# Attention scores of later token groups: two groups at once in four 64x64 tiles, values in the same visit

## The chip, the cores and the metric

The kernel runs on one core of one Trainium2 chip. The metric is the device time of one execution in microseconds (us); the time before is the median of three runs. The profile comes from one more execution, taken by the hardware profiler.

## The reference

Window attention, then two gated feed-forward layers, all in float32. Queries and keys come as 4 batches x 8 heads x 576 positions x 64 numbers; a query sees itself and the 63 positions before it.

```python
scores = scale * np.matmul(q, k.transpose(0, 1, 3, 2))
mask = (rel >= 0) & (rel < window)          # window = 64
scores = np.where(mask, scores, -1000000000.0)
attn = np.exp(scores - np.max(scores, axis=-1, keepdims=True))
attn = attn / (np.sum(attn, axis=-1, keepdims=True) + 1e-09)
x = np.matmul(attn, v)                      # 2304 tokens x 512
x = (h * sigmoid(1.702 * h)) @ w_out        # h = x @ w_in, 2048 wide
out = (silu(xn @ w_gate) * (xn @ w_val)) @ w_o2   # xn = x / rms * rms_g, 1536 wide
```

## The kernel before

The 2304 tokens are 36 groups of 64. A group's queries see two blocks of 64 keys: the group's own and the one before it. Heads are taken in four pairs, so a group's scores are a tile of 128 rows (two heads x 64 queries) by 4 x 128 columns (four head pairs, 128 keys each).

Stage A (to about 425 us) holds the attention and the first feed-forward layer. The tokens go in six blocks of 512, 256 and four times 384. For each block there are 16 steps; step c multiplies the block by 128 columns of `w_in` (`up`, L652 to L654) and the result by 128 rows of `w_out` (`down_t`, L737 to L739). Each operand is split into a high and a low part in a reduced float32 form, so a product is three matmuls. Stage B is the second layer (from L1071 on, to the end of the program).

The attention of groups 0 to 7 (block 0) stands at the start. That of groups 8 to 35 is strewn between the steps of the block before the one that needs it. For each such group `attention` issues:

- the scores (L490): four matmuls in full float32, 128 x 128 into 128 columns. To get two heads from one matmul, the queries are stored as a block-diagonal matrix, half of it zeros: 64 rows of one head against 64 columns, 64 rows of the other against the other 64. The profile counts each such matmul as two instructions, since full float32 goes in two half passes, each with its own weight load.
- on VectorE the mask (L517) and the row maximum (L522), on ScalarE the exponentials (L527), on VectorE the inverse sums, on GpSimd or ScalarE the normalising product;
- the turning of the weights: for groups below 18 by TensorE transposes (L545), from 18 on by VectorE's transpose (L573) and copies of 32 x 32 blocks.

`values` (L619) then multiplies two groups' weights with their values: 16 matmuls of 128 x 64 into 64 columns, head one to the lower 64 output rows, head two to the upper ones. From its bank ScalarE makes the high part of x and VectorE the low part (L631), which `up` reads.

TensorE's output lives in 8 banks: four accumulators `y0` to `y3`, two in a ring `bank` (for `up`), two in a ring `abank` (scores, transposes, values, row sums). A ring gives out its tiles in turn, each when its last user is done.

The order of all instructions is made before the run: every operation is handed to `Planner.op` with a cost for each engine that could do it, its dependences and a priority (in steps of stage A). `Planner.emit` walks a simulated time and writes down which operation each engine takes next. Costs of going from one form of matmul to another are in `Planner.TURN` (r: reduced float32, f: full float32, v: values). On the chip each engine then runs its list in that order and waits on semaphores. SyncE issues most loads, in its list's order. The weights arrive as float64 and are made float32 by VectorE and ScalarE (`w_narrow`, L391 to L405), and then split (`w_split`, L436) in stage A.

Of the kernel before, what the change touches and what calls it, by code (L numbers as in the profile page):

```python
# [9 lines left out]
F32 = mybir.dt.float32  # L10
F32R = mybir.dt.float32r
# [31 lines left out]
class Planner:  # L43
# [180 lines left out]
def dma(nbytes):  # L224
    c = Load(0.45)
    c.size = nbytes
    return c
# [3 lines left out]
def window_attention_two_moe_kernel(ctx: ExitStack, tc: tile.TileContext, ins, out):  # L231
    nc = tc.nc
    qh, kh, vh, w_in, w_out, w_gate, w_val, w_o2, rms_g = ins
    NBAT, NBLK = qh.shape[0], qh.shape[1]
    NT, DM = out.shape
# [80 lines left out]
    pl = Planner({k: v[1] for k, v in KINDS.items()})  # L316

    pts = [at.tile([P, NK, P], F32, name=f"pts{i}") for i in range(2)]
    KS = 8
# [8 lines left out]
    def make(b):  # L328
        if b.kind == "pt":
            turn = pt_turn[0] = 1 - pt_turn[0]  # L330
            b.tile = pts[turn]
            return b.tile
        if b.kind in mix_turn:
# [110 lines left out]

    q_of, kw, vw, vals = {}, {}, {}, []
    starts = [("keys", n) for n in range(KS // 2)]

    def wkey(g):
        b, i = divmod(g, NBLK)
        return b, max(i - 1, 0)  # L450

    def load_q(g, prio, kind="q", by="D"):
        b, i = divmod(g, NBLK)
        t = q_of[g] = Buf(kind)
        pl.op({by: dma(P * 2048)}, lambda e: (nc.scalar if e == "A" else nc.sync).dma_start(out=make(t), in_=qh[b, i]),
              prio, new=[t], size=P * 2048)

    def load_k(g, prio, kind="k"):
        if wkey(g) in kw:
            return  # L460
        b, i = wkey(g)
        t = Buf(kind)
        kw[b, i] = (lambda: t.tile), [t]
        pl.op({"D": dma(P * 2048)}, lambda e: nc.sync.dma_start(out=make(t), in_=kh[b, :, i:i + 2]), prio, new=[t])

# [14 lines left out]
    def attention(g, p0, step, ekind="e", ptkind="pt", norm=("G",), ptev=("A", "V"), hi=("A",)):  # L480
# [70 lines left out]
        if g < NS:  # L551
            pl.op({"T": 1.2}, masked_scores, p0, r=[*qk, "mask", "negative", "ident", *extra],
                  w=["scores order"], new=[sb],
                  mode="f")
            pl.op({"V": dve(512)}, highest_of, p0, r=[sb], new=[nb])
# [33 lines left out]
        return g, v, pb, [v, pb, "at", *extra] + (nov if g >= NPE else []), hi  # L589

    turns = {}
    idle = Buf("y2")
    idles = []

    def stay_warm(n, after):
        first = not idles

        def fn(e):
            t = make(idle) if first else idle.tile
            for _ in range(n):  # L600
                nc.tensor.matmul(t[:, 0:P], warm, warm, start=True, stop=True)

        idles.append(pl.op({"T": 0.25 * n}, fn, -70, r=["warm", START], after=[after], mode="f",
                           **({"new": [idle]} if first else {"hold": [idle]})))
# [786 lines left out]
    warm = start.tile([P, P], F32, name="warm")  # L1391
    n_first = start.tile([P, 1, P], F32R, name="n_first")
    n_rest = start.tile([P, 1, P], F32R, name="n_rest")
    ident_r = start.tile([P, P], F32R, name="ident_r")
    first_exp = start.tile([P, 1], F32, name="first_exp")
# [19 lines left out]
    pl.op({"G": 0.1}, lambda e: nc.gpsimd.memset(mhalf, -0.5), -97, w=["mhalf"])  # L1415

    def load_k_start(i, prio):
        tok = starts[i // 2]
        pl.op({"D": dma(P * 2048)}, lambda e: nc.sync.dma_start(out=k_start[:, i:i + 2], in_=kh[0, :, i:i + 2]), prio, w=[tok])

# [104 lines left out]
    plans.sort()  # L1525
    parts, pending = [], []
    pi = 0
    bi = 0
    for s in range(SA):
        j, c = steps[s]  # L1530
        while pi < len(plans) and plans[pi][0] <= s:
            p, g = plans[pi]
# [9 lines left out]
        while pending and s >= first[next(i for i in range(NBA) if gbase[i] + ngrp[i] > pending[0][0][0][0]) - 1]:  # L1542
            values(*pending.pop(0))
        gs, o = a_up(j, c, s)
# [88 lines left out]
```

## Time and profile before

| | us |
|---|---|
| median of three runs | 903.09 (902.3 to 903.85) |
| the profiled execution | 902.74 |
| its span, first to last instruction | 901.0 |
| TensorE busy in the span | 892.7 |
| VectorE busy | 677.5 |
| ScalarE busy | 446.8 |
| GpSimd busy | 287.6 |

A matmul's line names its output tile, then its operands, the shape of the weights and that of the result. Matmuls overlap in the profile: a busy time of one is longer than the distance from its start to the next start, so distances between starts are what a matmul costs in a dense stream. Idle time of TensorE is listed with what ended it.

### The profile page before, as it was taken

The page shows a single profiled execution, that of the slowest core. Times are in us where ns is not written, and L with a number is a line of the kernel's source. Part 1 is how long each engine was busy: PE and PEld are TensorE (multiplying, and loading weights), DVE is VectorE, ACT ScalarE, POOL GpSimd, SP SyncE. Part 2 cuts the span into 40 slices and gives each one's busy share as a digit, 9 for nine tenths or more (in the row PEclk, how much of TensorE's full clock was granted, in tenths as well). Part 3 has the DMA queues.
Part 4 walks back from the last instruction along what each step waited for, and adds up shares of the span by engine and source line. Part 5 has one row for each costly group of instructions (what it writes and reads, how often), then busy time and mean ns, then how long its engine had stood idle before and what let it go on. Part 6 is the DMA issues. An engine that isn't in the chain of part 4 may idle for free.

```text
span 901.0 us, 15907 instructions
## 1 busy us (share of the span) xinstructions
PE 892.7 (99%) x5656; PEld 845.6 (94%) x5656; DVE 677.5 (75%) x1320; ACT 446.8 (50%) x1106; POOL 287.6 (32%) x414
## 2 busy tenths in 40 slices
PE   9999999999999999999999999999999999999998
PEld 8888889999999999999999999998999999999998
DVE  6999986667657666764459888888787867677896
ACT  7975665566655666564337444444432224322251
POOL 4211212243444444541002543233222224233440
PEclk9999999999999999999999999999999999999999
DMA  9952455636556455533356999999998879988992
GB/s 333 394 200 75 124 190 182 233 120 223 199 182 208 158 177 158 190 136 117 133 189 245 347 348 337 328 327 285 377 369 268 259 202 296 287 248 234 260 226 71
DMA packets 96020, 208.03 MB, mean 231 GB/s; under 512 B 8754, under 2 KB 45380, under 8 KB 94404
## 3 DMA queue, kind: packets, MB, share of 16 engines
q1 hardware_dynamic: 68148, 145.40, 46.2%
q0 software_dynamic: 27648, 61.35, 23.4%
q8 instruction: 45, 0.74, 0.3%
q14 instruction: 35, 0.29, 0.1%
q10 hardware_dynamic: 144, 0.26, 0.1%
HBM read 147.20 MB, written 59.78 MB: 230 GB/s over the span
## 4 chain that ended last, share of the span: by engine, by line
PE 91%; DVE 4%; ACT 3%; DMA 1%; issue 1%; POOL 0%; SPq 0%; POOLq 0%; DVEq 0%; ACTq 0%
PE bank L1071 9%; PE bank L1072 9%; PE bank L1073 9%; PE y L737 7%; PE y L739 7%; PE y L738 7%; PE bank L652 7%; PE bank L653 7%; PE bank L654 7%; PE abank L490 3%; PE y L1346 2%; PE y L1345 2%; PE y L1347 2%; PE abank L619 2%; PE abank L1345 1%; PE abank L1346 1%
## 5 line engine op out<-in xcount | busy, mean ns | idle before, releaser
L1071 PE MATMUL bank<-slab,slab 128*128 128x384 f32 x456 | 154.6, 339 | 0.8 <-DVE gh L1110 0.8
L1072 PE MATMUL bank<-slab,slab 128*128 128x384 f32 x456 | 153.7, 337 | 0.8 <-DVE slab L931 0.8
L1073 PE MATMUL bank<-slab,slab 128*128 128x384 f32 x456 | 153.5, 337 | 0.0
L737 PE MATMUL y<-gh,slab 128*128 128x384 f32 (+2 forms) x384 | 132.0, 344 | 0.4 <-DVE y L761 0.4
L739 PE MATMUL y<-gh,slab 128*128 128x384 f32 (+2 forms) x384 | 129.1, 336 | 0.0
L652 PE MATMUL bank<-xh,slab 128*128 128x384 f32 (+2 forms) x380 | 128.9, 339 | 0.2 <-DVE mix L720 0.2
L738 PE MATMUL y<-gl,slab 128*128 128x384 f32 (+2 forms) x384 | 129.0, 336 | 0.0
L654 PE MATMUL bank<-xh,slab 128*128 128x384 f32 (+2 forms) x380 | 127.9, 336 | 0.0
L653 PE MATMUL bank<-xl,slab 128*128 128x384 f32 (+2 forms) x380 | 127.8, 336 | 0.0
L960 POOL DMA_DIRECT2D slab<-wc x96 | 55.7, 581 | 179.0 <-PE bank L1073 173.6
L1071 PEld LDWEIGHTS bank<-slab,slab 128*128 128x128 f32 x456 | 85.6, 188 | 8.7 <-DVE gh L1110 2.8
L1072 PEld LDWEIGHTS bank<-slab,slab 128*128 128x128 f32 x456 | 85.7, 188 | 5.9 <-DVE slab L931 1.0
L720 DVE SCALAR_TENSOR_TENSOR mix<-mix,bank 128x384 f32<-128x384 f32 (+2 forms) x95 | 52.1, 549 | 49.2 <-ACT mix L716 48.7
L1073 PEld LDWEIGHTS bank<-slab,slab 128*128 128x128 f32 x456 | 85.6, 188 | 0.0
L716 ACT ACTIVATE mix<-bank 128x384 f32<-128x384 f32 (+2 forms) x95 | 46.3, 488 | 78.9 <-PE bank L654 77.4
L1110 DVE TENSOR_TENSOR gh<-gl,bank 128x384 f32<-128x384 f32 x108 | 59.2, 550 | 24.9 <-PE bank L1073 24.2
L737 PEld LDWEIGHTS y<-gh,slab 128*128 128x128 f32 x384 | 72.2, 188 | 3.5 <-DVE y L761 0.6
L739 PEld LDWEIGHTS y<-gh,slab 128*128 128x128 f32 x384 | 72.1, 188 | 2.7
L738 PEld LDWEIGHTS y<-gl,slab 128*128 128x128 f32 x384 | 72.2, 188 | 2.5
L652 PEld LDWEIGHTS bank<-xh,slab 128*128 128x128 f32 x380 | 71.5, 188 | 3.2 <-DVE mix L720 0.5
L654 PEld LDWEIGHTS bank<-xh,slab 128*128 128x128 f32 x380 | 71.4, 188 | 2.7
L653 PEld LDWEIGHTS bank<-xl,slab 128*128 128x128 f32 x380 | 71.5, 188 | 2.6
(240 smaller groups left out, 2000.4 us busy)
## 6 DMA issues: line engine op xcount, KB each, us to landing
slab<-wc POOLq DMA_DIRECT2D x72, 512.0 KB, 5.1
wc<-slab SPq DMA_DIRECT2D x36, 512.0 KB, 6.0
wp<-raw SPq DMA_DIRECT2D x24, 512.0 KB, 3.6
fw<-wp SPq DMA_DIRECT2D x12, 1024.0 KB, 8.4
q<-in_q_dram SPq DMA_DIRECT2D x35, 256.0 KB, 4.6
raw<-in_w_in_dram SPq DMA_DIRECT2D x16, 512.0 KB, 8.2
raw<-in_w_out_dram SPq DMA_DIRECT2D x16, 512.0 KB, 6.5
k<-in_k_dram SPq DMA_DIRECT2D x25, 256.0 KB, 3.7
```

Of the source, the lines that this page charges most:

```text
L652: nc.tensor.matmul(h, w[:, 0, kk], xh_ring[:, kk, at_], start=(kk == 0), stop=False)
L653: nc.tensor.matmul(h, w[:, 0, kk], xl_ring[:, kk, at_], start=False, stop=False)
L654: nc.tensor.matmul(h, w[:, 1, kk], xh_ring[:, kk, at_], start=False, stop=(kk == NK - 1))
L720: nc.vector.scalar_tensor_tensor(out=th, in0=th, scalar=1.0, in1=hb.tile[:, 0:n], op0=ALU.add, op1=ALU.mult)
L737: nc.tensor.matmul(y, s[:, 0, cols], hb.tile[:, 0:n], start=first, stop=False)
L738: nc.tensor.matmul(y, s[:, 0, cols], lb.tile[:, 0:n], start=False, stop=False)
L739: nc.tensor.matmul(y, s[:, 1, cols], hb.tile[:, 0:n], start=False, stop=last)
L960: pl.op({"G": 0.6}, lambda e: nc.gpsimd.dma_start(out=frame(f)[:, :, 0:n], in_=d), prio, r=[key], w=tok, size=P * 8 * n)
L1071: nc.tensor.matmul(h, w[:, 0, kk], xh[:, kk], start=kk == 0, stop=False)
L1072: nc.tensor.matmul(h, w[:, 0, kk], xl[:, kk], start=False, stop=False)
L1073: nc.tensor.matmul(h, w[:, 1, kk], xh[:, kk], start=False, stop=kk == 1)
L1110: nc.vector.tensor_tensor(out=(make(to) if kind else s.tile)[:, 0:HT].bitcast(F32), in0=s.tile[:, 0:HT].bitcast(F32), in1=b.tile[:, 0:HT], ...
```

## The change

Groups 8 to 35 are no longer taken one by one but as 14 pairs (g, g + 1), g even.

- **Queries.** They come dense, not block-diagonal: 64 rows hold the even heads of the pairs, 64 rows the odd heads. One load of 256 KB brings both groups (before 256 KB for each), and one of 384 KB the three key blocks that a pair needs (before 256 KB per group, shared by two groups where a batch begins).
- **Scores.** 16 matmuls of 64 x 64 into 128 columns replace eight of 128 x 128. Even heads use array rows 0 to 63 and write to one `abank`, odd heads rows 64 to 127 and write to the other, so that a pair holds both banks. Four tiles of the array take turns in the order (row half, column half) = (0,0), (1,1), (0,1), (1,0).
- **After the scores** each bank (four heads of both groups, 128 x 512) runs through the same chain as a group did before: mask, maximum, exponentials, inverse, product, transposes. The counts on VectorE, ScalarE and GpSimd stay, but for first groups of a batch, whose mask is now two instructions of half the size where only one group of the pair is first, and for eight block copies fewer.
- **Values** are 16 matmuls of the same form as before, into a `bank` instead of an `abank`. Their priority is set just behind the scores of the next pair, and a new form "s" (scores) in `TURN` lets the planner put both into one visit.
- **Loads.** Values are loaded for every group (28 loads of 256 KB; before, two groups at a batch's start shared one). The first pair's queries and keys wait for the last scores of the start (`opened`). There is one buffer for the pair's queries and one for its keys.
- The first pair is planned three steps later; masks of the start move into unused columns of `xl_ring`.

```diff
-    TURN = {("r", "v"): 0.071, ("f", "v"): 0.071, ("v", "r"): 0.233, ("v", "f"): 0.18}
+    TURN = {("r", "v"): 0.071, ("f", "v"): 0.071, ("v", "r"): 0.233, ("v", "f"): 0.18, ("r", "s"): 0.071, ("f", "s"): 0.071,
+            ("s", "r"): 0.233, ("s", "f"): 0.18, ("v", "s"): 0.071, ("s", "v"): 0.071}
...
-        "q": (at, 2, [P, NK, 2 * W], F32),
-        "k": (at, 1, [P, 2, NK, W], F32),
+        "q": (None, 2, [P, NK, 2 * W], F32),
+        "qq": (None, 1, [P, NK, 2 * W], F32),
+        "k": (None, 1, [P, 3, NK, W], F32),
...
-        "e": (at, 1, [P, NK, P], F32),
+        "e": (None, 2, [P, NK, P], F32),
...
+    def load_pair(g, prio):
+        t = q_of[g] = Buf("qq")
+        pl.op({"D": dma(P * 2048)}, lambda e: nc.sync.dma_start(
+            out=make(t).rearrange("p k c -> p (k c)"), in_=qp[g // 2].rearrange("p i k c -> p (i k c)")), prio, new=[t], after=opened)
+        t2 = k_of[g] = Buf("k")
+        pl.op({"D": dma(P * 3072)}, lambda e: nc.sync.dma_start(out=make(t2), in_=kh[:, g - 1:g + 2]), prio, new=[t2], after=opened)
...
+    def attention_pair(g, p0, step, norm=("G",), ptev=("A", "V")):
+        q, kb = q_of.pop(g), k_of.pop(g)
+        banks, es = [Buf("abank") for _ in range(2)], [Buf("e") for _ in range(2)]
...
+            for i in range(2):
+                for h in range(2):
+                    for lane, half in ((0, 0), (1, 1), (0, 1), (1, 0)):
+                        rows, p = slice(lane * W, (lane + 1) * W), 2 * h + half
+                        nc.tensor.matmul(to[lane][half * W:(half + 1) * W, (2 * i + h) * P:(2 * i + h + 1) * P],
+                                         qt[rows, i, p], kb.tile[rows, i:i + 2, p], start=True, stop=True)
+
+        pl.op({"T": 1.0}, scores, p0, r=[q, kb], w=["scores order"], new=[*banks, *es],
+              after=[vals[NS - 1], idles[-1]], mode="s")
+        chains = [half_chain(g, lane, p0, step, banks[lane], es[lane], firsts, norm, ptev) for lane in range(2)]
+        return g, v_of.pop(g), chains
...
+    def values_pair(part, prio):
+        g0, vs, chains = part
+        ob = Buf("bank")
...
+                        pt = chains[j][0].tile[:, 2 * i + p // 2, p % 2 * W:(p % 2 + 1) * W]
+                        nc.tensor.matmul(o[rows, (p * 2 + i) * W:(p * 2 + i + 1) * W], vt, pt, start=True, stop=True)
...
     def plan(j, s0, s1):
-        for i in range(ngrp[j]):
-            plans.append((s0 + i * (s1 - s0) / ngrp[j], gbase[j] + i))
+        n = ngrp[j] // 2
+        for i in range(n):
+            plans.append((s0 + i * (s1 - s0) / n, gbase[j] + 2 * i, s0 + (i + 1) * (s1 - s0) / n - 0.28))
...
-        plan(j, first[j - 1] - 2, first[j] - 2)
+        plan(j, first[j - 1] - (2 if j > 1 else -1), first[j] - 2)
...
-            load_q(g, p - 4)
-            load_k(g, p - 4)
-            if wkey(g) not in vw:
-                load_v(g, p - 3, ("v", "t1" if g < NPE else "vx")[len(vw) % 2], ups[-2:-1])
-            parts.append(attention(g, p - 0.3, 1.7, norm=("A", "G") if g < gbase[2] else ("G",)))
-            if g % 2:
-                pending.append((parts, p - 0.3 + 2.5))
-                parts = []
+            load_pair(g, p - 4)
+            load_values(g, pv - 5, ("v", "t1" if g < NPE else "vx"), ups[-2:-1])
+            pending.append((attention_pair(g, p - 0.3, 1.7, norm=("A", "G") if g < gbase[2] else ("G",)), pv))
```

What this does to the order is shown at three places. A row is a line, an operation, output<-operands and the output's shape; "waits" names whose semaphores the instruction waits for.

**TensorE at the end of the start**, from the values of group 7 to the first matmuls of `up`. Before (L619 values, L490 scores of group 8, L652 to L654 `up`):

```order
L619 MATMUL abank<-pts_88,v_467 64x64 [waits DMAHW7_49,Activation_49]
L619 MATMUL abank<-pts_88,v_467 64x64 x7
L490 MATMUL abank<-k,q 128x128 [waits DMAHW6_49,DMAHW4_49,DVE_49]
L490 MATMUL abank<-k,q 128x128 x3
L652 MATMUL y_531<-xh,slab_510 128x256 [waits Activation_49]
L653 MATMUL y_531<-xl,slab_510 128x256 [waits DVE_49]
```

and of the changed kernel (L769 values, L638 the scores of the pair 8, 9, L802 to L804 `up`):

```order
L769 MATMUL abank<-pts_92,v_463 64x64 [waits DMAHW6_49,DVE_49]
L769 MATMUL abank<-pts_92,v_463 64x64 x7
L638 MATMUL abank<-kq,q 64x128 [waits DMAHW3_49,DMAHW4_49,DVE_49,PE_49]
L638 MATMUL abank<-kq,q 64x128 [waits DVE_49]
L638 MATMUL abank<-kq,q 64x128 x14
L802 MATMUL y_527<-xh,slab_506 128x256 [waits Activation_49]
L803 MATMUL y_527<-xl,slab_506 128x256
```

The second score matmul, the first that writes to the second bank, has a wait on VectorE of its own, and `up` behind it no longer has one.

**VectorE at the same place.** Before (L631 is the low part of x of groups 6 and 7, L405, L395 and L399 convert weights, L517 is the mask of group 8):

```order
L631 TENSOR_TENSOR xl<-abank,xh 128x4x64 [waits Activation_49]
L405 SCALAR_TENSOR_TENSOR raw_430<-raw_430 128x512 [waits DVE_49]
L395 TENSOR_SCALAR raw_495<-raw_495 128x512 [waits DMAHW1_49]
L395 TENSOR_SCALAR raw_514<-raw_514 128x512 [waits DMAHW2_49]
L399 SCALAR_TENSOR_TENSOR raw_495<-raw_495 128x512 [waits DVE_49]
L631 TENSOR_TENSOR xl<-abank,xh 128x4x64 [waits Activation_49]
L517 SCALAR_TENSOR_TENSOR e<-abank,m_rest 128x512 [waits PE_49]
```

and of the changed kernel (L781 low parts, L424 and L418 conversions, L653 the mask of the pair's first bank):

```order
L781 TENSOR_TENSOR xl<-abank,xh 128x4x64 [waits Activation_49]
L1590 TENSOR_SCALAR gcol<-gcol 128x4 [waits DMAHW1_49]
L424 SCALAR_TENSOR_TENSOR raw_410<-raw_410 128x512 [waits DVE_49]
L418 SCALAR_TENSOR_TENSOR raw_437<-raw_437 128x512
L781 TENSOR_TENSOR xl<-abank,xh 128x4x64 [waits Activation_49]
L653 SCALAR_TENSOR_TENSOR es_89<-abank,m_rest 128x256 [waits PE_49]
L653 SCALAR_TENSOR_TENSOR es_89<-abank,m_first 128x256
L424 SCALAR_TENSOR_TENSOR raw_437<-raw_437 128x512 [waits DVE_49]
```

The low part of group 7 keeps its place, and the mask stands right behind it in both, with weight conversions behind the mask.

**TensorE inside a block of 384.** Before, a value visit with one group's scores behind it (the other group's scores stand alone some 50 rows later):

```order
L654 MATMUL bank<-xh,slab_1116 128x384
L619 MATMUL abank<-pts_89,mix 64x64 x8
L619 MATMUL abank<-pts_88,v 64x64 x8
L490 MATMUL abank<-k,q 128x128 x4
L737 MATMUL y_2505<-gh,slab_1147 128x384
```

and of the changed kernel (L723 values, of which 16 rows of this kind follow each other, four shown; L887 `down_t`):

```order
L804 MATMUL bank<-xh,slab_1028 128x384
L638 MATMUL abank<-kq,q 64x128 x16
L723 MATMUL bank<-pts_93,v 64x64
L723 MATMUL bank<-pts_92,v 64x64
...
L723 MATMUL bank<-pts_93,mix 64x64
L723 MATMUL bank<-pts_92,mix 64x64
L887 MATMUL y_2528<-gh,slab_1076 128x384
```

All of a pair's scores now stand in one place. Of the 14 pairs' score visits, eight have a value visit right behind them as here; six stand alone, the first pair's among them, and six value visits stand alone. The order of stage B is the same in both kernels.

## Rows read from the trace of the kernel before

**Rows 1.** The page's busy times and granted TensorE clock over 40 slices

```profile
PE 892.7 (99%) x5656; PEld 845.6 (94%) x5656; DVE 677.5 (75%) x1320; ACT 446.8 (50%) x1106; POOL 287.6 (32%) x414
...
PEclk9999999999999999999999999999999999999999
```

**Rows 2.** Waits of TensorE, 0 to 425 us: total us, times, longest; first and last

```profile
PE y L1403 <- DVE warm L1396: 1.0, 1, 1.0
...
PE bank L652 <- DVE mix L720: 0.2, 1, 0.2
```

**Rows 3.** The line of the scores: count, least, median and longest duration in ns

```profile
L490 PE MATMUL abank<-k,q x224: 270/275/377, 29.4 to 391.5; 128*128 128x128 f32 x112
```

**Rows 4.** Timeline of TensorE around one score visit: start, busy, line, form, count

```profile
109.50 0.39 PE L739 MATMUL y<-gh,slab 128*128 128x512 f32 x1
109.72 1.05 PE L490 MATMUL abank<-k,q 128*128 128x128 f32 x8
...
110.85 0.39 PE L653 MATMUL bank<-xl,slab 128*128 128x512 f32 x1
111.08 0.39 PE L654 MATMUL bank<-xh,slab 128*128 128x512 f32 x1
```

**Rows 5.** Timeline of TensorE around one value visit

```profile
99.89 0.39 PE L654 MATMUL bank<-xh,slab 128*128 128x512 f32 x1
100.21 0.69 PE L619 MATMUL abank<-pts,v 128*64 128x64 f32 x16
100.72 0.64 PE L619 MATMUL abank<-pts,t 128*64 128x64 f32 x16
...
101.63 0.40 PE L738 MATMUL y<-gl,slab 128*128 128x512 f32 x1
```

**Rows 6.** Timeline of a value visit behind which a score visit stands

```profile
164.20 1.16 PE L490 MATMUL abank<-k,q 128*128 128x128 f32 x8
165.12 0.36 PE L652 MATMUL bank<-xh,slab 128*128 128x256 f32 x1
```

**Rows 7.** TensorE's timeline cut at 100.24 and 100.345 us (values), 109.75 and 109.85 us (scores)

```profile
100.21 0.28 PE L619 MATMUL abank<-pts,v 128*64 128x64 f32 x2
...
100.21 0.34 PE L619 MATMUL abank<-pts,v 128*64 128x64 f32 x4
...
109.72 0.27 PE L490 MATMUL abank<-k,q 128*128 128x128 f32 x1
...
109.72 0.38 PE L490 MATMUL abank<-k,q 128*128 128x128 f32 x2
```

**Rows 8.** Timeline of TensorE at the end of the start

```profile
29.45 1.16 PE L490 MATMUL abank<-k,q 128*128 128x128 f32 x8
30.84 0.38 PE L652 MATMUL y<-xh,slab 128*128 128x256 f32 x1 [0.24 <-ACT xh L356]
31.46 0.38 PE L653 MATMUL y<-xl,slab 128*128 128x256 f32 x1 [0.23 <-DVE xl L631]
31.68 0.28 PE L654 MATMUL y<-xh,slab 128*128 128x256 f32 x1
31.80 0.28 PE L652 MATMUL y<-xh,slab 128*128 128x256 f32 x1
...
32.85 0.39 PE L652 MATMUL bank<-xh,slab 128*128 128x512 f32 x1
```

**Rows 9.** Timeline of VectorE from there on

```profile
30.98 0.42 DVE L631 TENSOR_TENSOR xl<-abank,xh 128x256 fp32r<-128x256 f32 x1
31.31 0.69 DVE L517 SCALAR_TENSOR_TENSOR e<-abank,m_rest 128x512 f32<-128x512 f32 x1
...
35.79 0.69 DVE L436 TENSOR_TENSOR slab<-raw,slab 128x512 fp32r<-128x512 f32 x1
```

**Rows 10.** Timeline of TensorE: the first matmul that reads the slab of 35.79 us

```profile
39.72 0.48 PE L737 MATMUL y<-gh,slab 128*128 128x512 f32 x1
```

**Rows 11.** Busy time by stage: span, PE, PEld, DVE, ACT, POOL (counts in brackets)

```profile
30.00:60.00 30.00, 29.44 (x169) 23.82 (x168) 29.62 (x57) 26.63 (x62) 6.59 (x5) 1.00 0.79 310
```

More of the change, by code (lines that the diff above doesn't have):

```diff
@@ L316, in window_attention_two_moe_kernel @@
     pl = Planner({k: v[1] for k, v in KINDS.items()})
+    es = [at.tile([P, NK, P], F32, name=f"es{i}") for i in range(2)]
+    e_turn = [1]
+    q_turn = [0]
+    q_tile = at.tile([P, NK, 2 * W], F32, name="q")
+    kq_tile = at.tile([P, 3, NK, W], F32, name="kq")
     pts = [at.tile([P, NK, P], F32, name=f"pts{i}") for i in range(2)]
@@ L331, in make @@
             b.tile = pts[turn]
+            return b.tile
+        if b.kind == "q":
+            q_turn[0] = 1 - q_turn[0]
+            b.tile = q_tile if q_turn[0] else kq_tile[:, 0:2].rearrange("p i k c -> p (i k c)").rearrange("p (k c) -> p k c", k=NK)
+            return b.tile
+        if b.kind in ("qq", "k"):
+            b.tile = q_tile if b.kind == "qq" else kq_tile
+            return b.tile
+        if b.kind == "e":
+            turn = e_turn[0] = 1 - e_turn[0]
+            b.tile = es[turn]
             return b.tile
@@ L454, in load_q @@
         t = q_of[g] = Buf(kind)
-        pl.op({by: dma(P * 2048)}, lambda e: (nc.scalar if e == "A" else nc.sync).dma_start(out=make(t), in_=qh[b, i]),
+        pl.op({by: dma(P * 2048)}, lambda e: (nc.scalar if e == "A" else nc.sync).dma_start(out=make(t), in_=qh[i]),
               prio, new=[t], size=P * 2048)
@@ L463, in load_k @@
         kw[b, i] = (lambda: t.tile), [t]
-        pl.op({"D": dma(P * 2048)}, lambda e: nc.sync.dma_start(out=make(t), in_=kh[b, :, i:i + 2]), prio, new=[t])
+        pl.op({"D": dma(P * 2048)}, lambda e: nc.sync.dma_start(out=make(t), in_=kh[:, i:i + 2]), prio, new=[t])
     def load_v(g, prio, kind="v", after=()):
@@ new lines, in load_values, with scores @@
+    def load_values(g, prio, kinds, after=()):
+        v_of[g] = [Buf(kind) for kind in kinds]
+        for i, t in enumerate(v_of[g]):
+            pl.op({"D": dma(P * 2048)}, lambda e, i=i, t=t: nc.sync.dma_start(
+                out=make(t), in_=(vr if t.kind == "v" else vr.rearrange("s (k c) -> s k c", k=NK))[(g + i - 1) * W:(g + i + 1) * W]),
+                prio + i, new=[t], after=after)
+    def attention_pair(g, p0, step, norm=("G",), ptev=("A", "V")):
+        q, kb = q_of.pop(g), k_of.pop(g)
+        banks, es = [Buf("abank") for _ in range(2)], [Buf("e") for _ in range(2)]
+        firsts = [(g + i) % NBLK == 0 for i in range(2)]
+        def scores(e):
+            to = [make(b) for b in banks]
+            qt = q.tile.rearrange("p k c -> p (k c)").rearrange("p (i k c) -> p i k c", i=2, k=NK)
+            for i in range(2):
[8 more added lines that the diff above has]
+        return g, v_of.pop(g), chains
@@ new lines, in values_pair, with product, found, x_hi @@
+    def values_pair(part, prio):
+        g0, vs, chains = part
+        ob = Buf("bank")
+        cs = [(g * W) % RING // W for g in (g0, g0 + 1)]
+        def product(e):
+            o = make(ob)
+            for i, v in enumerate(vs):
+                for p in range(NK):
+                    for j in range(2):
+                        rows = slice(j * W, (j + 1) * W)
+                        vt = v.tile[:, p, rows] if v.kind in ("t1", "vx") else v.tile[:, p * P + j * W:p * P + (j + 1) * W]
+                        pt = chains[j][0].tile[:, 2 * i + p // 2, p % 2 * W:(p % 2 + 1) * W]
+                        nc.tensor.matmul(o[rows, (p * 2 + i) * W:(p * 2 + i + 1) * W], vt, pt, start=True, stop=True)
+        def found():
+            return ob.tile.rearrange("p (k c) -> p k c", k=NK)
+        cols = slice(xcols(g0).start, xcols(g0).start + 2 * W)
+        def x_hi(e):
+            copy(e, xh_ring[:, :, cols], found())
+        def x_lo(e):
+            nc.vector.tensor_tensor(out=xl_ring[:, :, cols], in0=found(), in1=xh_ring[:, :, cols].bitcast(F32),
+                                    op=ALU.subtract)
+        vals.append(pl.op({"T": 1.08}, product, prio, r=[*vs, "at", *(t for _, ts in chains for t in ts)], new=[ob], mode="v"))
+        pl.op({"A": act(512, False)}, x_hi, prio, r=[ob], w=[("xh", c) for c in cs])
+        pl.op({"V": dve(512)}, x_lo, prio, r=[ob, *(("xh", c) for c in cs)], w=[("xl", c) for c in cs])
@@ L1391, in window_attention_two_moe_kernel @@
     warm = start.tile([P, P], F32, name="warm")
-    n_first = start.tile([P, 1, P], F32R, name="n_first")
-    n_rest = start.tile([P, 1, P], F32R, name="n_rest")
-    ident_r = start.tile([P, P], F32R, name="ident_r")
+    n_first, n_rest, ident_r = xl_ring[:, 0:1, 512:640], xl_ring[:, 0:1, 640:768], xl_ring[:, 1, 512:640]
     first_exp = start.tile([P, 1], F32, name="first_exp")
@@ L1531, in window_attention_two_moe_kernel @@
         while pi < len(plans) and plans[pi][0] <= s:
[L1532 removed]
+            p, g, pv = plans[pi]
             pi += 1
[L1534 to L1543 removed]
+            load_pair(g, p - 4)
+            load_values(g, pv - 5, ("v", "t1" if g < NPE else "vx"), ups[-2:-1])
+            pending.append((attention_pair(g, p - 0.3, 1.7, norm=("A", "G") if g < gbase[2] else ("G",)), pv))
+        while pending and s >= first[next(i for i in range(NBA) if gbase[i] + ngrp[i] > pending[0][0][0]) - 1]:
+            values_pair(*pending.pop(0))
         gs, o = a_up(j, c, s)
```

85 lines of the change are left out of this document (73 added, 12 removed).

## The prediction

> **What bounds the kernel now.** The page's busy times come first: TensorE is busy 99% of the span, no other engine over 75%, and the clock row shows the full level, 2.4 GHz, in every slice [rows 1]. The list of TensorE's waits is next: in the 425 us of stage A the longest is 1.0 us, at the very start, the shortest of the list's eight rows 0.2, and together they are 3.3 us [rows 2]. So stage A is one stream of matmuls, and a change is worth what it takes out of that stream, as long as no new wait comes in. The third view is TensorE's timeline, for distances between starts.
>
> A score visit: the last regular matmul starts at 109.50, the second one behind the visit at 110.85, which is 1.35 us; two regular steps of this size are 2 x 0.23 (110.85 to 111.08), so the visit lengthens the stream by 0.89 [rows 4]. Where it stands behind a value visit it takes the same, 164.20 to 165.12 [rows 6]. 224 instructions at 8 a visit are 28 visits [rows 3], 24.9 us. A value visit in the same way: 99.89 to 101.63 is 1.74, less 0.46 is 1.28 [rows 5].
>
> **What four tiles cost.** A full-float32 matmul goes in two half passes. The trace has no matmul that uses half of the array's rows, so the new price is bounded from two sides.
>
> In the score visit of before one half pass starts every 0.11 us (the busy stretch grows from 0.27 to 0.38 with the second) [rows 7]; eight fill the visit, and its 0.89 holds everything. In the value visit, whose matmuls use half of the columns, two half passes have started after the first 0.04 us and four at 0.345 [rows 7]: they come in twos, on two tiles. From four (0.34) to sixteen (0.69) the stretch grows by 0.35 in six steps, 0.058 a step [rows 5, 7]. Thirty-two half passes are 16 steps, 0.93 us. The other 0.35 of the 1.28 is what it costs to get into this form of matmul and out of it.
>
> The new visit has 32 half passes (16 matmuls) of 128 columns. Four at a time they are 8 steps of 0.11, 0.89 us, the time of a single group's scores before. Low end: 0.89 without any change of form. High end: two at a time, 16 x 0.11 = 1.78, plus 0.35. I take four at a time, because the value row shows tiles that don't wait for each other, and add 0.35 for the change of form where the visit stands alone: **1.24**. Where values follow at once, the way out of one form is the way into the next; I take half of 0.35, between nothing and all of it: **1.07**.
>
> **The sum over pairs 2 to 14.** They remove 26 visits: 26 x 0.89 = 23.1 us. They add 5 visits alone and 8 joined: 5 x 1.24 + 8 x 1.07 = 14.8. Value visits keep form and number, transposes too. That is 8.3 us less.
>
> **The first pair is another matter.** Before, the scores of group 8 (29.45) lie in a hole: `up` behind them waits for x, its first matmul starts at 30.84, its second at 31.46, and the next `up` at 32.85 [rows 8]. The visit is free there. The pair now needs two `abank` tiles, and the second is freed only by the low part of group 7, which VectorE ends at 30.98 + 0.42 = 31.40 [rows 9]. Only then do the scores go on: 31.4 + 0.89 + 0.17 = 32.5, and 12 matmuls of 0.12 (31.68 to 31.80) put the next `up` at 33.9, 1.0 later than 32.85 [rows 8]. Group 9's own visit of 0.89 goes. Net 0.1 us more. Queued behind that wait on TensorE is `up`; on VectorE the mask, which started at 31.31, now starts after 32.4, and the weight conversions behind it wait about 1 us. VectorE has nothing to give there, 29.62 of 30 us busy [rows 11]. The cover is the lead of the weights: the slab that VectorE ends at 35.79 + 0.69 = 36.5 is first read at 39.72, 3.2 us later [rows 9, 10]. If that cover were gone, the whole 1 us would show.
>
> **Costed at nothing.** VectorE, ScalarE and GpSimd keep their counts; split masks and eight copies fewer are under 2 us on engines that are not the bound. Query and key loads get fewer, two a pair, of 640 KB together, for up to four of 256 KB. A pair's loads wait for the scores of the pair before; visits reach from 29.4 to 391.5 us [rows 3], so pairs are 28 us apart on average, and that is their lead. What is queued behind them on SyncE's list are weights, whose lead is the one above. Values now take a tile of `bank` from `up`; the next `up` needs the tile of the `up` before, and between them stand 12 matmuls of `down_t` at 0.12 to 0.23 [rows 4, 8] and the visit's 2.3 us, at least 3.7 us, against two passes over one tile, of 0.7 us each on VectorE [rows 9]. Stage B has the same order and moves as a whole.
>
> Total: 8.3 - 0.1 = 8.2 us. From the profiled execution's 902.74 that gives 894.5; the median of the runs is 0.35 higher, so I write **894.9**. With the bounds: joined visits at 0.89 or 1.24 are 1.4 us either way; if half passes can't be issued faster than the two in 0.058 us of the value visit [rows 5, 7], 32 take 0.93 and not 0.89, 0.5 us more over 13 visits; new waits are 0 to 2 us. The likeliest case's own range is 893 to 899.
>
> **Rivals.**
>
> *Two tiles at a time.* The two half passes of one matmul follow each other on the same tile, and the instructions stand in the order half 1, half 2 of one tile, then of the next. If TensorE kept to that order, the first half pass of the second tile could start only beside the second of the first, and never more than two would run: 1.78 a pair. Then 5 x 2.13 + 8 x 1.95 = 26.3 against 23.1, 3.2 us more, and the first pair 0.1 + 0.89 = 1.0 more: 4.2 us, **907.3, slower**. It decides from 1.48 us of pure scores a pair (14 of them plus 5 x 0.35 + 8 x 0.17, less 0.8 at the start, equal 23.1). For it: no row shows more than two tiles at work, and none shows half the rows. Against it: in the value visit two half passes have started in the first 0.04 us [rows 7], where that order would allow one. By the Trainium skill, TensorE: Matmul & The Clock Gate, section The mechanism, matmuls start and end in program order without reordering, which would give this rival's 907.3; the trace's two starts at once do not agree with it. Chance 0.14.
>
> *The gain is eaten by waits.* VectorE is full from 30 us on [rows 11], and TensorE gains on it. If the leads melt, or block borders wait for x, the first block's gain and some 2 us at borders go: about 8.2 - 4 = 4 us, 899. For it: the 1 us that VectorE loses at the start; against it: a lead of 3 us against a gain of under 1 us in that block. Chance 0.10.
>
> *No tiles overlap.* The change then doesn't do what it says: 32 x 0.11 = 3.5 a pair, 14 of them plus 3.1 less 0.8, against 23.1: 28 us more, 931. The twos of rows 7 speak against it, though they show columns only. Chance 0.03.
>
> **How the numbers follow.** The forecast has 0.73 and gives 894.9. No change is within 0.2% of 903.1, 1.8 us, about what a measurement of this kernel can tell. Forecast and eaten gain lie below 901.3, but for a small part: faster 0.79. Cases between them and the slower rivals: same 0.05. Two tiles or none overlapping: slower 0.16. The range takes in the likeliest case's own and most of the eaten gain, 892.5 to 901.0; it leaves out the slower rivals.
>
> **What would show it.** Right: score visits behind which the regular matmul starts 1.1 to 1.3 us later than a dense stream would; at a cut 0.04 us into one, four half passes started; on TensorE's wait list one wait of about 1.5 us near 30 us for VectorE's low part, and else a list like before; stage B as long as before. Wrong: a step of 0.11 us with two half passes, thus visits of 2 us; or waits of TensorE for slabs between 35 and 125 us, or for x where a block begins.

## The result, and the profile after

The changed kernel takes **893.33 us** (median of 4 executions, 891.66 to 895.36) beside 903.33 us for the kernel before, measured on the same chip: a ratio of 0.9892, 95% interval 0.9869 to 0.9914. The forecast was 894.9 us. Measured once more, beside later experiments, it took 892.80 us (4 executions, 892.57 to 893.01, ratio 0.9896 [0.9880, 0.9911]). The profile of that later measurement is called the second profile below, and the one of here the first. Of the six executions of the run with a bank from the `up` ring (below), two ran at a granted clock of 0.75 and 0.56 (1073.92 and 1445.29 us) and are left out of its figures.

The page of the changed kernel, first profile (busy time, share of the span, instructions; the granted clock in 40 slices), answers to [rows 1]:

```profile
PE 882.9 (99%) x5880; PEld 833.4 (93%) x5880; DVE 675.6 (76%) x1341; ACT 444.6 (50%) x1091; POOL 270.5 (30%) x405
...
PEclk9999999999999999999999999999999999999999
```

TensorE has 224 matmul instructions more (the profile counts half passes; it is 112 matmuls) and is busy 9.8 us less; it is still the stream that sets the time. The clock row is a mean over slices of 22 us, so a fall of the clock that lasts 3 us, as below, does not show there. The list of its waits in the first 425 us (total, times, longest) answers to [rows 2]:

```profile
PE abank L638 <- DVE xl L781: 1.1, 1, 1.1
PE y L1551 <- DVE warm L1544: 1.0, 1, 1.0
...
PE abank L769 <- DVE pts L377: 0.5, 1, 0.5
PE abank L769 <- ACT pts L375: 0.4, 1, 0.4
```

Line 638 holds the scores. One wait is new, the first row, and it is the one that was forecast for the first pair. The values of the start (L769) wait 0.9 us for their weights where they waited 0.5; the two rows not shown (0.5 and 0.3) are as before. Stage A lasts longer than the 425 us named above: stage B's first matmul starts at 477.15 us before and at 467.95 now, and TensorE has no wait between 425 us and there in either. Next, TensorE's timeline (start, busy, line, tiles, form, count): a score visit alone, answering to [rows 4], then one with values behind it, answering to [rows 5, 6]. L802 to L804 are `up`, L887 to L889 `down_t`, L723 the values.

```profile
100.18 0.40 PE L804 MATMUL bank<-xh,slab 128*128 128x512 f32 x1
100.51 1.10 PE L638 MATMUL abank<-kq,q 64*64 64x128 f32 x32
...
101.88 0.40 PE L888 MATMUL y<-gl,slab 128*128 128x512 f32 x1
102.12 0.39 PE L889 MATMUL y<-gh,slab 128*128 128x512 f32 x1
...
292.76 0.34 PE L804 MATMUL bank<-xh,slab 128*128 128x384 f32 x1
293.03 1.10 PE L638 MATMUL abank<-kq,q 64*64 64x128 f32 x32
294.06 0.69 PE L723 MATMUL bank<-pts,v 128*64 128x64 f32 x16
294.58 0.64 PE L723 MATMUL bank<-pts,mix 128*64 128x64 f32 x16
...
295.43 0.34 PE L888 MATMUL y<-gl,slab 128*128 128x384 f32 x1
```

Alone: 100.18 to 101.88 is 1.70, less two regular steps (0.47) is **1.23** for two groups. Joined: 292.76 to 295.43 is 2.67, less two steps of 0.175 is 2.32; without the value visit's 1.28 that is **1.04**. A pair took 2 x 0.89 before. That all four tiles start together is seen where the timeline is cut 0.02 us into the first of these visits:

```profile
100.51 0.34 PE L638 MATMUL abank<-kq,q 64*64 64x128 f32 x4
```

Now the first pair, at the end of the start (answers to [rows 8]). Before, the last values of the start, from which the distances below are counted, began here:

```profile
28.83 0.69 PE L619 MATMUL abank<-pts,v 128*64 128x64 f32 x16 [0.25 <-ACT pts L356]
```

and in the first profile of the changed kernel:

```profile
28.92 0.69 PE L769 MATMUL abank<-pts,v 128*64 128x64 f32 x16 [0.47 <-DVE pts L377]
29.53 0.43 PE L638 MATMUL abank<-kq,q 64*64 64x128 f32 x2
31.03 1.44 PE L638 MATMUL abank<-kq,q 64*64 64x128 f32 x30 [1.07 <-DVE xl L781]
32.41 0.58 PE L802 MATMUL y<-xh,slab 128*128 128x256 f32 x1
...
35.10 0.39 PE L802 MATMUL bank<-xh,slab 128*128 128x512 f32 x1
```

The first matmul of the even heads runs (two half passes), the second needs the odd heads' bank, and all stand still for 1.07 us until VectorE has taken the low part out of it. The next `up` of 512 columns starts at 35.10, where it was 32.85 [rows 8]. Most of these 2.25 are not the wait: the busy times of the rows behind it are those of a lower clock. By stretch (span, then PE, PEld, DVE, ACT, POOL busy, granted clock, DMA share, GB/s):

```profile
31.00:35.00 4.00, 3.97 (x42) 3.64 (x43) 2.50 (x6) 1.59 (x3) 1.15 (x1) 0.58 1.03 412
...
32.20:34.20 2.00, 2.00 (x14) 1.80 (x9) 1.70 (x5) 0.31 (x1) 0.00 (x0) 0.50 1.02 410
```

The second profile has the same standstill to the hundredth, and no fall of the clock:

```profile
30.14 0.69 PE L769 MATMUL abank<-pts,v 128*64 128x64 f32 x16 [0.47 <-DVE pts L377]
30.76 0.43 PE L638 MATMUL abank<-kq,q 64*64 64x128 f32 x2
32.26 1.10 PE L638 MATMUL abank<-kq,q 64*64 64x128 f32 x30 [1.07 <-DVE xl L781]
33.28 0.38 PE L802 MATMUL y<-xh,slab 128*128 128x256 f32 x1
...
34.80 0.39 PE L802 MATMUL bank<-xh,slab 128*128 128x512 f32 x1
```

The granted clock of that profile over the same stretch, 1.00, in the same columns as above:

```profile
31.00:35.00 4.00, 2.93 (x45) 2.56 (x44) 2.81 (x8) 2.43 (x5) 1.31 (x1) 1.00 1.03 411
```

**Where the 9.5 us went** (profiled executions, 902.74 to 893.29). Pairs 2 to 14: 26 x 0.89 = 23.1 before, 5 x 1.23 + 8 x 1.04 = 14.5 now, 8.6 less. The first pair: `up` 2.25 later (0.1 of it because the start itself took longer), group 9's own visit of 0.89 gone, 1.4 more. Two waits of stage A where a block begins are gone, for VectorE's `y` (0.4) and for its `mix` (0.2, the last of [rows 2]), together 0.6. From the first matmul of stage B to the end it is 0.3 less. That makes 8.1; some 1.3 us of shorter gaps in stage A are not assigned.

### The profile page after: what moved, and what is told of

It is laid out like the page before. It is cut to its first block, busy times and chain, and to the rows that moved or that the text cites. A ratio compares the mean times of both kernels' runs of the same rounds, so it can differ in the third digit from the quotient of the medians.

```text
span 891.5 us, 16252 instructions
## 1 busy us (share of the span) xinstructions
PE 882.9 (99%) x5880; PEld 833.4 (93%) x5880; DVE 675.6 (76%) x1341; ACT 444.6 (50%) x1091; POOL 270.5 (30%) x405
## 4 chain that ended last, share of the span: by engine, by line
PE 95%; DVE 3%; ACT 1%; issue 0%; POOL 0%; DVEq 0%; POOLq 0%
PE bank L1221 10%; PE bank L1222 9%; PE bank L1223 9%; PE y L887 8%; PE bank L802 8%; PE y L889 8%; PE y L888 7%; PE bank L803 7%; PE bank L804 7%; PE y L1496 2%; PE y L1495 2%; PE y L1497 2%; PE bank L723 2%; PE abank L638 2%; PE abank L1495 1%; PE abank L1496 1%
## 5 line engine op out<-in xcount | busy, mean ns | idle before, releaser
L887 PE MATMUL y<-gh,slab 128*128 128x384 f32 (+2 forms) x384 | 131.1, 341 | 0.0
L802 PE MATMUL bank<-xh,slab 128*128 128x384 f32 (+2 forms) x380 | 129.2, 340 | 0.0
L889 PE MATMUL y<-gh,slab 128*128 128x384 f32 (+2 forms) x384 | 129.2, 336 | 0.0
L804 PE MATMUL bank<-xh,slab 128*128 128x384 f32 (+2 forms) x380 | 127.8, 336 | 0.0
L887 PEld LDWEIGHTS y<-gh,slab 128*128 128x128 f32 x384 | 72.1, 188 | 3.7 <-issue 0.5
L802 PEld LDWEIGHTS bank<-xh,slab 128*128 128x128 f32 x380 | 71.5, 188 | 3.4 <-issue 0.3
L889 PEld LDWEIGHTS y<-gh,slab 128*128 128x128 f32 x384 | 72.1, 188 | 2.6
L804 PEld LDWEIGHTS bank<-xh,slab 128*128 128x128 f32 x380 | 71.4, 188 | 2.7
```

The costliest lines, as they stand in the source:

```text
L802: nc.tensor.matmul(h, w[:, 0, kk], xh_ring[:, kk, at_], start=(kk == 0), stop=False)
L804: nc.tensor.matmul(h, w[:, 1, kk], xh_ring[:, kk, at_], start=False, stop=(kk == NK - 1))
L887: nc.tensor.matmul(y, s[:, 0, cols], hb.tile[:, 0:n], start=first, stop=False)
L889: nc.tensor.matmul(y, s[:, 1, cols], hb.tile[:, 0:n], start=False, stop=last)
```

## The experiments

Theory: the gain is four tiles at work at once, and the first pair gives some back. The rivals are about how TensorE chooses what runs side by side, what the joint visit is worth, and whether VectorE or the standstill sets the first block. Times are medians, ratios are to the kernel before on the same chip.

### Four in a row on each tile

```diff
-            for i in range(2):
-                for h in range(2):
-                    for lane, half in ((0, 0), (1, 1), (0, 1), (1, 0)):
+            for lane, half in ((0, 0), (1, 1), (0, 1), (1, 0)):
+                for i in range(2):
+                    for h in range(2):
```

> The change, but with the 16 score matmuls of a pair ordered tile by tile: the four matmuls of one 64x64 tile in a row, then those of the next tile. Same work, same place in the stream. Theory 1 (a half pass may overtake others that wait for their own tile, but only those right ahead of it): eight half passes of one tile now stand in a row, nothing behind them gets past, and a pair's 32 half passes run nearly one after another: 32 x 0.11 = 3.5 us in place of 0.89, 14 pairs, about 37 us more than the change, near 930 us. Theory 2 (TensorE looks far ahead in its queue and feeds every free tile): visits stay at 1.23 us and the time at 893.

Measured: 912.03 us, 1.0099 [1.0084, 1.0113], slower than before. A visit alone takes 2.70 (101.10 to 104.27, less 0.47):

```profile
101.10 0.40 PE L804 MATMUL bank<-xh,slab 128*128 128x512 f32 x1
101.43 2.56 PE L638 MATMUL abank<-kq,q 64*64 64x128 f32 x32
...
104.27 0.40 PE L888 MATMUL y<-gl,slab 128*128 128x512 f32 x1
...
101.43 0.65 PE L638 MATMUL abank<-kq,q 64*64 64x128 f32 x4
...
101.43 0.81 PE L638 MATMUL abank<-kq,q 64*64 64x128 f32 x6
```

The last two rows are cuts at 101.88 and 101.93: half passes start singly up to the fourth, and the fifth brings a sixth with it. At one half pass a step on each tile, the sixth belongs to the second tile. So the second tile begins with the third matmul of the first tile, ahead of the three half passes of that tile that still wait. The time lies between the two expectations: tiles overlap, but only where one ends and the next begins. 13 x 1.47 = 19.1 us more is what the visits give, and 18.7 over 893.33 is what was measured.

### Lane by lane, and half by half

```diff
-            for i in range(2):
-                for h in range(2):
-                    for lane, half in ((0, 0), (1, 1), (0, 1), (1, 0)):
+            for lane in range(2):
+                for i, h in ((0, 0), (0, 1), (1, 0), (1, 1)):
+                    for half in range(2):
```

> The change, but with all matmuls of the even heads first (array rows 0 to 63, the two column halves in turn), then all of the odd heads. Theory 1 (the whole gain is that four tiles run at once): two at a time, 16 steps of 0.11 = 1.78 us, visits of 2.1 us; 14 x 0.89 = 12.5 us more than the change, about 905.8 us, so slower than the kernel before. In the first pair the even heads' matmuls need no wait, which gives up to 0.9 us back. Theory 2 (the gain comes from dense queries, fewer loads and the shared visits): time stays within 2 us of 893.

Measured: 898.63 us, 0.9951 [0.9937, 0.9966]. Alone 1.72, joined 2.80. At cuts of 100.47 and 100.52 in a visit that begins at 100.00 eight and twelve half passes have started, so twos, and then a four:

```profile
100.00 0.65 PE L638 MATMUL abank<-kq,q 64*64 64x128 f32 x8
...
100.00 0.83 PE L638 MATMUL abank<-kq,q 64*64 64x128 f32 x12
```

The second lane begins with the fifth half pass of each of the first lane's tiles. It goes ahead of six half passes that stand before it in the list, three of each tile. Neither theory has this time: the first is right about the twos, but it forecast visits of 2.1 and 905.8 us because it left out the stretch of fours. 13 x 0.49 is 6.4; the total is 5.3 over 893.33. The 1.1 between them is not assigned: at the first pair the next `up` of 512 columns comes 4.65 behind the last start values, 1.5 earlier than in the first profile of the changed kernel, but no earlier than in the second. The same with the other pairing, tiles that write the same half of the rows first:

```diff
+            for half in range(2):
+                for i, h in ((0, 0), (0, 1), (1, 0), (1, 1)):
+                    for lane in range(2):
```

> Kept: one visit per pair, same 32 matmuls, banks and layout. Changed: the order, the two tiles that write the same half of the rows of their banks first (even and odd lane by turns, 16 matmuls), then the other two. Theory 1 (any two of the four tiles run side by side, as the two halves of one lane did, where a visit alone took 1.72 us): alone 1.7, joined 2.8, total about 5.5 us over the changed kernel, 898.5. Theory 2 (two tiles that write the same half of the rows do not run side by side): alone towards 2.7 as tile by tile, total towards 912.

Measured: 899.40 us, 0.9957 [0.9941, 0.9972]. Alone 1.72 (100.23 to 102.42, less 0.47), joined 2.80:

```profile
100.23 0.40 PE L804 MATMUL bank<-xh,slab 128*128 128x512 f32 x1
100.56 1.59 PE L638 MATMUL abank<-kq,q 64*64 64x128 f32 x32
...
102.42 0.40 PE L888 MATMUL y<-gl,slab 128*128 128x512 f32 x1
```

The first theory holds (the visits give 13 x 0.49 = 6.4, the total is 6.1 over 893.33): two tiles run side by side in either pairing, and the gain comes from the order that turns to another tile with every matmul. The same 32 half passes cost 1.23, 1.72 and 2.70 us in three orders.

### The values apart from the scores

```diff
-s0 + (i + 1) * (s1 - s0) / n - 0.28))
+s0 + (i + 1) * (s1 - s0) / n - 1.28))
```

> Kept: four tiles at once, one visit for two groups. Changed: the values are planned earlier, so that in the trace all values of pairs 2 to 14 should stand apart from the scores (in the changed kernel 8 of these 13 visits are joined). Theory 1 (a joined visit costs 1.04 us on top of a value visit's 1.28, one that stands alone 1.23, so joining is worth 8 x 0.19 = 1.5 us): about 894.8. Theory 2 (joining is worth nothing, all of the gain is the four tiles): 893.3, within 0.5.

Measured: 895.32 us, 0.9925 [0.9912, 0.9937], 2.5 over the changed kernel's 892.80 on the same chip. In the trace all 14 value visits and 13 score visits stand alone, at 1.28 and 1.24 us; 8 joints at about 0.2 are 1.6. The rest is partly two waits that the changed kernel has not:

```profile
PE y L887 <- ACT slab L375: 0.3, 1, 0.3
PE y L887 <- DVE y L911: 0.2, 1, 0.2
```

The other 0.4 is not assigned; from about 67 us on, the order of all the work differs too. The first theory holds by the visits: "values in the same visit" is a part of the gain of its own, about 1.6 of it.

### The standstill at the first pair

Three kernels take it away or fill it. The first puts the odd heads of that pair alone in a tile of the `up` ring:

```diff
-        banks, es = [Buf("abank") for _ in range(2)], ...
+        banks, es = [Buf("bank" if g == NS and lane else "abank") for lane in range(2)], ...
```

> The change, but the first pair's odd heads write to a tile of the ring bank, which is free, and not to the second abank, which the low part of x of group 7 still reads. Theory 1 (the first pair loses 1.1 us to that wait and about as much again because TensorE's granted clock falls to half after it, 0.58 from 31 to 35 us): the wait of 1.07 us goes from the list, the clock stays at 1.00, the next up starts at 32.4 to 32.9 us and not 35.1, and the kernel takes 2.2 to 2.7 us less than the change, about 891. Theory 2 (the hole is there anyway, since up waits for x): under 0.5 us less.

Measured: 895.03 us (median of four), 0.9911 [0.9896, 0.9927], some 2 us more than the changed kernel, where both theories expected less. At the first pair it does what it should: from the last start values to the next `up` of 512 columns 3.5 us, where the second profile has 4.66 (30.14 to 34.80). It also shows the starts one by one, since two kinds of banks take turns:

```profile
30.27 0.32 PE L638 MATMUL abank<-kq,q 64*64 64x128 f32 x1
30.28 0.32 PE L638 MATMUL bank<-kq,q 64*64 64x128 f32 x1
30.28 0.32 PE L638 MATMUL abank<-kq,q 64*64 64x128 f32 x1
30.29 0.32 PE L638 MATMUL bank<-kq,q 64*64 64x128 f32 x1
30.43 0.27 PE L638 MATMUL abank<-kq,q 64*64 64x128 f32 x1
```

But the order of the work behind it came out another way, and TensorE waits for VectorE between 33 and 125 us, where the changed kernel has no such row:

```profile
PE bank L802 <- DVE mix L870: 1.3, 2, 0.7
PE y L888 <- DVE gl L827: 0.4, 1, 0.4
```

The second fills the wait with idle matmuls:

```diff
+    stay_warm(5, vals[-1])
```

> The change, with five more idle matmuls of 128 x 128 on a spare bank between the values of group 7 and the first pair's scores, so that the wait is filled but stays. Theory 1 (half of the first pair's loss is the clock, which fell because TensorE stood still): the scores still start at about 31.0 us, the granted clock stays at 1.00, the next up starts at about 33.5 us and not 35.1, 1.6 us less than the change, about 891.7. Theory 2 (the clock falls for another reason, or the fall costs nothing): no difference above 0.5 us.

Measured: 893.35 us, 0.9890 [0.9874, 0.9907], the clock at 1.00 throughout, the next `up` 4.67 us behind the last start values. That is 1.5 earlier than in the first profile, as expected, and no earlier than in the second, which has no filling. The total is the changed kernel's (893.33 and 892.80), as theory 2 has it; but here too the order of the work behind it differs, and TensorE waits 0.7 us for VectorE's `mix` between 33 and 125 us. The third turns the order of this one pair:

```diff
+            if g == NS:
+                turns_.sort(key=lambda x: x[2])
```

> Kept: everything but the order of the 32 matmuls of the first pair of groups (those in the start), which run even heads first and then odd heads, so that the first 16 do not need the second bank. Theory 1 (the standstill of 1.07 us and the half clock behind it cost 1.4 us, and filling it gives that back): clock near 1.00 from 31 to 35 us, the next up-projection of 512 columns about 1.5 us earlier behind the last start value than in the changed kernel (6.18 us there), total about 891.9. Theory 2 (VectorE is full in the first block and holds TensorE up there instead): the same up-projection earlier, but new waits for VectorE between 35 and 100 us that add up to about as much; total within 0.4 us of the changed kernel, 893.3.

Measured: 892.42 us, 0.9892 [0.9879, 0.9906], 0.4 under the changed kernel's 892.80, about what the executions of either spread over. Its first pair:

```profile
30.03 1.09 PE L640 MATMUL abank<-kq,q 64*64 64x128 f32 x16
31.53 1.09 PE L640 MATMUL abank<-kq,q 64*64 64x128 f32 x16 [0.41 <-DVE xl L783]
32.55 0.39 PE L804 MATMUL y<-xh,slab 128*128 128x256 f32 x1
```

The wait falls from 1.07 to 0.41, but two tiles at a time the matmuls take twice 1.09: 32.55 - 30.03 is 2.52, and the second profile has 33.28 - 30.76 = 2.52 as well. Theory 2 has the right total and not the right reason, as there are no new waits. My premise fell: the half clock is not what that standstill always brings.

### VectorE in the first block

```diff
-            for a, n in ((0, NK),) if firsts[0] == firsts[1] else ((0, 2), (2, 2)):
+            for a, n in (...) * (4 if g == NS and lane else 1):
```

> Kept: everything. Added: the mask of the first pair's odd bank is multiplied in four times instead of once (zeros and ones, so the result stays), about 2.0 us more of VectorE near 32 us. Theory 1 (VectorE has slack in the first block of the changed kernel and takes it up): no more than 0.4 us, 893.3 to 893.7. Theory 2 (VectorE is what TensorE follows in the first block): the 2.0 us show in full, new waits for VectorE between 35 and 100 us that add up to about 2 us, total about 895.3.

> The changed kernel once more, on the chip of the other three runs, as the mark for differences of 1 to 2 us: 893.3, within 1 us if chips and executions differ no more than they did so far.

Measured: 894.91 us, 0.9918 [0.9904, 0.9931], against 892.80 for the changed kernel once more: 2.1 us for 2.0 added. New waits between 33 and 125 us:

```profile
PE bank L802 <- DVE mix L870: 0.8, 1, 0.8
PE y L888 <- DVE gl L827: 0.5, 1, 0.5
```

Theory 2 holds; the waits add up to 1.3 us and not 2, in an execution that at 893.95 was the fastest of its four. The order of TensorE's list is the changed kernel's. In the changed kernel TensorE has no wait between 33 and 135 us, and yet VectorE has nothing to spare there: it is just in time. So I tried to relieve it, by taking six low halves of weights on GpSimd:

```diff
-        w_split(key, i, prio, home=home, lo=("V",) if n < 1 else ("G", "V"))
+        w_split(key, i, prio, home=home, lo=("V",) if n < 1 else ("G",) if 3 <= n < 9 else ("G", "V"))
```

> Kept: the changed kernel's attention. Changed: the low halves of the fourth to ninth narrow weight block are taken on GpSimd alone, which takes 6 operations of 0.68 us off VectorE in the first block (4.1 us) and puts as many of 1.32 us on GpSimd; one score visit fewer is joined (0.2 us). Theory 1 (VectorE is full in the first block but just in time, TensorE has no wait there, so relief alone gives nothing): within 0.5 us of the changed kernel, 892.8. Theory 2 (VectorE still paces TensorE there): up to 4 us less, about 889. Either falls if the low halves come too late from GpSimd: waits for POOL slab between 35 and 100 us.

> The relief of VectorE and, of the first pair, the odd heads' bank from the ring of the up-projection, so that the standstill of 1.07 us before the first pair is gone. Theory 1 (that bank gives 1.15 us at the first pair, and VectorE ate it; relieved, it does not): no waits for VectorE between 60 and 125 us, total about 891.8, 1.1 us under the same kernel without that bank. Theory 2 (the waits come from where that bank puts the work, not from VectorE being full): waits for DVE mix and gl stay near 1 us or more, total 893 or more.

> The relief of VectorE (4.1 us) and the mask of the first pair's odd bank four times (2.0 us more), which by itself cost 2.1 us. Theory 1 (what counts is how much VectorE has to do in the first block): the relief covers it, within 0.5 us of the relieved kernel, 892.8. Theory 2 (it is the place near 32 us that counts, where the work stands ahead of the first slabs): 2 us over the relieved kernel, 894.8.

Measured: relieved 897.30 us (0.9937 [0.9918, 0.9955]), with the bank of the first pair as well 896.11 (0.9922 [0.9905, 0.9938]), with four masks 899.28 (0.9957 [0.9940, 0.9973]). The relief costs 4.5 us, which neither theory gave, and not through late low halves, since TensorE has no wait for GpSimd's slabs. The waits of TensorE in the relieved kernel between 33 and 125 us:

```profile
PE bank L802 <- DVE mix L870: 2.7, 3, 1.7
```

The relieved kernel with four masks has the same row with 2.8. This profile is of an execution of 899.85 us, 2.6 over the median, whose clock fell behind the standstill. Its busy times by stretch, and under them those of the changed kernel's first profile, whose clock fell too:

```profile
31.00:35.00 4.00, 3.48 (x37) 3.15 (x38) 1.94 (x6) 1.56 (x4) 1.30 (x1) 0.57 1.02 409
...
30.00:60.00 30.00, 28.92 (x183) 23.30 (x180) 26.06 (x45) 24.92 (x58) 11.17 (x8) 0.94 0.77 298
60.00:90.00 30.00, 27.62 (x145) 21.17 (x144) 29.77 (x55) 18.29 (x44) 7.61 (x6) 1.00 0.26 98
```

```profile
30.00:60.00 30.00, 28.97 (x154) 23.99 (x155) 27.64 (x55) 25.46 (x59) 5.31 (x4) 0.94 0.84 331
60.00:90.00 30.00, 30.00 (x190) 24.31 (x189) 29.11 (x56) 19.70 (x46) 4.95 (x4) 1.00 0.17 58
```

GpSimd took the work (5.31 to 11.17 us), and VectorE stood idle for 3.9 us from 30 to 60 instead of 2.4, to be full from 60 to 90, when TensorE loses 2.4. What it was spared early it did not use; the planner had put its list in another order. The waits and the joint that is missing are 2.9 of the 4.5; the rest is not assigned. The added masks again show in full (899.28 - 897.30 = 2.0), as the second theory of that run says. The bank gives 1.2 on top of the relief (897.30 - 896.11), near the 1.1 that was expected, though the intervals overlap and its waits are of other kinds (1.5 us for ScalarE's slab, 1.1 for GpSimd). Whether the bank's gain in the unrelieved kernel is lost to VectorE's amount of work or to its order stays open. No version here beats the changed kernel by more than the executions spread.

## Why the prediction was right, and where it was not

**Four at a time** is right, and the rival with two at a time is out: four half passes have started at the cut, 32 of them fit into a visit of 1.23 (forecast 1.24), and the same half passes in orders that leave tiles idle take longer: 1.72 where they run in twos with a stretch of fours, 2.70 tile by tile. The Trainium skill, TensorE: Matmul & The Clock Gate, section The mechanism, says that matmuls start and end in program order. Of whole matmuls that agrees with the rows of the run with a bank from the `up` ring, where four starts follow each other within 0.02 us (30.27 to 30.29). Of half passes it does not, since a tile's second half pass comes behind the others' first (30.43), and on that reading my 907.3 rested. And the runs in other orders show a matmul for another tile starting ahead of one for a busy tile that stands before it (tile by tile, the sixth start, between 101.88 and 101.93).

**0.35 for the change of form** is right where the visit is alone (1.23 - 0.89 = 0.34). Joined, I took half of it, 0.17, and measured 1.04 - 0.89 = 0.15. One reading on the way there was wrong and changed nothing: "four at 0.345" is the time of the cut, 100.345, which lies 0.14 us into the visit; the 0.34 that the sum goes on from is the busy time of that row. The sum over pairs 2 to 14 was 8.3, measured 8.6.

**The first pair** is the term that was mis-sized. The wait came where it was forecast, for the low part that VectorE ends, and 1.07 long instead of about 1.5. The scores go on 2.1 us behind the last start values (28.92 to 31.03), where the forecast had 2.6 (28.83 to 31.40 [rows 9]). Forecast was an `up` 1.0 later and net 0.1 more. Behind the last start values that `up` comes after 4.02 before, after 6.18 in the first profile and after 4.66 in the second. The first is 2.16 later, less 0.89 thus 1.3 us lost, and the half clock behind the standstill is 1.5 of it. The second is 0.64 later, less 0.89, thus 0.25 us gained. The step that failed is the count at full clock, and beside it VectorE's end, taken about 0.5 too late; that it can go either way was not in the bounds.

**Costed at nothing:** loads, transposes, the ring of `bank` show no wait of TensorE from 36 us to the end of stage A, as forecast. VectorE's lead was read too kindly: the 3.2 us between a slab and its first use [rows 9, 10] do not protect the block, since 2.0 us more of VectorE cost 2.1. "The gain is eaten by waits" names a mechanism that the runs with more work on VectorE show; in the changed kernel itself none of it shows.

**Stage B** was forecast as long as before, and its 0.3 less is inside what two executions differ by. The 1.3 us of stage A that are not assigned, and the 0.6 of waits that are gone at block borders, were not in my sum either. That the total came within 1.6 us of the forecast is therefore partly luck: the first pair's loss and these gains went opposite ways.

## What to carry to other kernels

Small matmuls that use different parts of the array run side by side only if those for the other tiles stand close by in the program; the same 32 half passes cost 1.23, 1.72 or 2.70 us by their order alone, so write the innermost loop over tiles. Put visits with small tiles next to each other, because the way out of one form and into the next is paid at every border (0.15 instead of 0.34 us beyond the scores' own 0.89). And an engine that is just in time shows no waits: add 2 us to it, and see whether they show, before you count its slack.

## What the runs showed of the hardware that was not expected

- After the same standstill of 1.06 or 1.07 us, which followed the same matmuls, TensorE's clock fell in two of seven profiled executions to the 1.2 GHz level (a mean of 0.58 and 0.57 from 31 to 35 us, the changed kernel's first profile and the relieved kernel) and stayed at 2.4 GHz (1.00) in the other five. What decides it, the runs don't show. With the wait filled it stayed full in the one profile there is.
- TensorE does not keep wholly to its list's order. With one tile's four matmuls in a row, the next tile begins with the third of them, ahead of three half passes that wait for the busy tile; lane by lane, the next lane goes ahead of six, three of each tile. So in these two runs the limit is three waiting half passes a tile, and not a distance in the list. It is too little to fill four tiles when a tile's four matmuls stand in a row; two in a row were not tried.
- Two tiles run side by side equally well whether they share the rows they read or the half of the rows they write: 1.72 us both ways.
